# Keys and queries loaded in runs of four rows, heads split over even and odd partitions

## The chip, the core and the metric

The kernel runs on one core of one Trainium2 chip. The metric is the device time of one execution in microseconds; the median of the runs shown is what counts. TensorE is PE in the profile, its weight loads are PEld, VectorE is DVE, ScalarE is ACT, GpSimd is POOL and SyncE is SP, which here does nothing but issue DMAs.

## What is computed

Attention with a narrow window and block summaries, then a mixture of experts with one expert for each token. Cut to what matters here:

```python
B, H, S, D = 4, 8, 768, 64            # q, k, v: [B, H, S, D], float32
block, window = 32, 16
k_sum = k.reshape(B, H, nb, block, D).max(axis=3)
scores_l = scale * q @ k.T             # kept where |i - j| < window
scores_s = scale * q @ k_sum.T + log(block)
a = softmax(concat(scores_l, scores_s))
x = a @ concat(v, v_sum)               # [B*S, H*D] = [3072, 512]
e = argmax(x @ w_gate)                 # one expert of 8 for each row
out = gate * sigmoid(x @ w_og)[e] * relu(x @ w1[e]) @ w2[e]
```

## The kernel before

**Tiling.** Attention runs over 24 tiles of 128 tokens, six for each of the four batch entries. Keys and queries are loaded 256 tokens at a time: twelve loads of keys and twelve of queries, 512 KB each, called `lk.n` and `lq.n` in the order table (n = 3b + u). A load (`load`, L343) puts tokens 2p and 2p+1 of all eight heads on partition p, so that one contiguous run in DRAM is two rows of 64 float32, 512 bytes. A copy on POOL, DVE or ACT (`reorder`, L352, `rk` and `rq`) brings the row index ahead of the head index.

**Turning.** Scores need keys and queries with the head dimension on partitions. `transposed` (L407, `pk` and `pq`) makes four PE transposes into one PSUM bank `pt` of shape 128 x 2 x 256: two head pairs, 256 tokens each. Bank g holds head pairs 2g and 2g+1. ACT or DVE then copy the bank into `KT` or `QT` (`keep_k` L416, `keep_q` L436, `kk` and `kq`), and DVE takes the maximum over each 32 keys (`max_k` L424, `mk`). Every load is turned in two banks, g = 0 and g = 1.

**Scores.** `scores` (L447, `sc`) walks over head pairs 0, 1, 2, 3; each takes four products of 64 queries with 120 columns of keys, which reach 32 columns into the next 64-token block.

**What sets the order.** The order of all attention work is written out by hand in the table `ORDER`: words are executed in turn, and each engine gets its instructions in that order. All loads of k, q and v, the stores of x to DRAM (`st`, L518) and later the weight loads stand in one queue, SP's. A DMA signals its landing on one of eight semaphores, dealt out in turn, and the ninth DMA after another on the same semaphore waits for that one to have landed. Raw keys have three buffers (`rawk`), raw queries two (`rawq`).

**Afterwards.** Expert work starts when the first lists of rows are made, at about 164 us in the profile, and takes the rest of the time. Weights come as 256 KB loads with runs of 2 KB (`raw`, 128 x 512).

Of the kernel before, what the change touches and what calls it, by code (L numbers as in the profile page):

```python
# [21 lines left out]
B, H, S, D = 4, 8, 768, 64  # L22
P = 128
HP = H // 2
# [3 lines left out]
KW = 88  # L28
PAD = 16
LW = 64  # L30
KTW = NB * KW + 2 * PAD
BANKS = "SsPpVvTM"
BUFS = {"mn": 4, "pr": 3, "pTe": 2, "pTl": 3, "xs": 4, "den": 3, "xT": 2, "ls": 2, "rawk": 3, "rawq": 2, "natk": 2, "natq": 1, "mst": 2, "km": 2, "lg": 2, "posi": 2, "y": 4}
RAWS = 5
# [12 lines left out]
SCALE = 1.0 / math.sqrt(D)  # L47
# [219 lines left out]
def in_bank(ps, bank, shape, name):  # L267
    return ps.tile(shape, F32, name=name, tag=f"bank{BANKS.index(bank)}", bufs=1)


def in_ring(pool, shape, name, tag, at, dt=F32):
    return pool.tile(shape, dt, name=name, tag=f"{tag}{at % BUFS[tag]}", bufs=1)
# [43 lines left out]
def attention(tc, const, sa, sb, st, ps, dr, q, k, v, id_sb, c_sb, wg_sb, x_dr, l_dr, rt, moe, table, begin, swap, presets):  # L316
    nc = tc.nc
    QT = [sb.tile([P, HP, 256], F32, name=f"qt{i}", tag=f"qt{i}", bufs=1) for i in range(2)]
    KT = [pool.tile([P, HP, KTW], F32, name=f"kt{i}", tag=f"kt{i}", bufs=1) for i, pool in enumerate((sa, sb))]
    VW = [pool.tile([W, NB, H, VP], F32, name=f"vw{i}", tag=f"vw{i}", bufs=1) for i, pool in enumerate((sa, sb))]  # L320
    MT = sa.tile([P, H, D], F32, name="mt", tag="mt", bufs=1)

    def clear(i, k, e):
        t, x = ((KT[i][:, :, 0:PAD], 0.0), (KT[i][:, :, KTW - PAD:KTW], 0.0), (VW[i][0:PAD, 0, :, 0:D], 0.0),
                (VW[i][96:W, NB - 1, :, 0:D], 0.0), (VW[i][:, :, :, D:D + 1], 1.0),
                (VW[i][LW:LW + NS, NB - 1, :, 0:D], 0.0), (VW[i][LW:W, NB - 4:NB - 1, :, 0:D], 0.0))[k]
        (nc.vector if e == "v" else nc.gpsimd).memset(t, x)

    def evac(dst, src, scale=None, engine="a"):
        if engine == "v" and scale is None:  # L330
            nc.vector.tensor_copy(dst, src)
        elif engine == "v":
            nc.vector.tensor_scalar(dst, src, scale, None, ALU.mult)
        else:
            nc.scalar.activation(dst, src, AF.Copy, scale=1.0 if scale is None else scale)
# [3 lines left out]
    def bank(shape, name):  # L339
        return in_bank(ps, banks_of.pop(0), shape, name)  # L340

    raws, nat = {}, {}

    def load(kind, b, u):
        src = {"k": k, "q": q}[kind]
        raw = in_ring(sa if kind == "k" else sb, [P, H, 2, D], f"raw_{kind}{b}{u}", "raw" + kind, 3 * b + u)
        nc.sync.dma_start(
            raw.rearrange("p h j d -> p h (j d)"),
            src[b, :, 256 * u:256 * (u + 1), :].rearrange("h (p j) d -> p h (j d)", j=2))
        raws[kind, b, u] = raw  # L350

    def reorder(kind, b, u, engine="p"):  # L352
        t = in_ring(sa if kind == "k" else sb, [P, 2, H, D], f"nat_{kind}{b}{u}", "nat" + kind, 3 * b + u)
        r = raws.pop((kind, b, u)).rearrange("p h j d -> p j h d")
        if engine == "a":
            nc.scalar.activation(t, r, AF.Copy)
        else:
            {"v": nc.vector, "p": nc.gpsimd}[engine].tensor_copy(t, r)
        nat[kind, b, u] = t
# [45 lines left out]
    ms, km, mps, banks = {}, {}, {}, {}  # L405

    def transposed(kind, b, u, g):  # L407
        n = nat[kind, b, u]
        pt = banks[kind, b, u, g] = bank([P, 2, 256], f"{kind}tr{b}{u}{g}")
        for x in range(2):  # L410
            hp = 2 * g + x
            for j in range(2):
                nc.tensor.transpose(pt[:, x, ds(j, P, 2)],
                                    n[:, j, 2 * hp:2 * hp + 2, :].rearrange("p h d -> p (h d)"), id_sb)

    def keep_k(b, u, g, e):  # L416
        pt = banks["k", b, u, g]
        at = PAD + 4 * u * KW
        src = pt.rearrange("p x (i s) -> p x i s", s=64)
        dst = KT[b % 2][:, 2 * g:2 * g + 2, at:at + 4 * KW].rearrange("p x (i w) -> p x i w", w=KW)  # L420
        evac(dst[:, :, :, 0:48], src[:, :, :, 0:48], engine=e)
        evac(dst[:, :, :, 48 + NS:KW], src[:, :, :, 48:64], engine=e)

    def max_k(b, u, g):  # L424
        if b not in km:
            km[b] = in_ring(sb, [P, HP, NS], f"km{b}", "km", b)
        nc.vector.tensor_reduce(out=km[b][:, 2 * g:2 * g + 2, 8 * u:8 * u + 8],
                                in_=banks["k", b, u, g].rearrange("p x (n s) -> p x n s", s=32), axis=AX.X, op=ALU.max)

    def k_sum(b, engine="p"):  # L430
# [3 lines left out]
            {"v": nc.vector, "p": nc.gpsimd}[engine].tensor_copy(own, km[b][:, hp, :].unsqueeze(1).to_broadcast([P, NB, NS]))  # L434

    def keep_q(b, u, g, e):  # L436
        evac(QT[(3 * b + u) % 2][:, 2 * g:2 * g + 2, :], banks["q", b, u, g], -SCALE, e)

    lg_sb = {}

# [204 lines left out]
    def key(f, kind=None):  # L645
        return (lambda s, *x: f(kind, s // 3, s % 3, *x)) if kind else (lambda s, *x: f(s // 3, s % 3, *x))

    work = {
        "cl": clear, "lk": key(load, "k"), "lq": key(load, "q"), "rk": key(reorder, "k"), "rq": key(reorder, "q"),
        "lv": lambda t, x, q: load_vw(*tiles[t], (x,), nc.gpsimd if q == "p" else nc.sync),  # L650
        "pk": key(transposed, "k"), "kk": key(keep_k), "mk": key(max_k), "pq": key(transposed, "q"), "kq": key(keep_q), "ks": k_sum,
        "me": means, "ke": keep_means, "mg": gather_means, "kg": keep_gathered, "pu": put_means,
        "sc": scores, "ma": mask, "mi": smallest, "su": subtract, "ex": exps, "tp": turn_p, "kp": keep_p, "va": values, "no": norm,
# [7 lines left out]
    for w in order:  # L661
        w, _, at = w.partition(":")
# [687 lines left out]
```

## Time and profile before

| | us |
|---|---|
| median of 3 runs | 498.84 |
| lowest and highest | 498.22 and 499.87 |
| profiled execution, its own time | 501.86 |
| its span, first to last instruction | 500.1 |
| PE busy in the span | 474.1 |
| DVE, ACT, POOL busy | 363.7, 313.7, 178.9 |

The profiled execution took 3.0 us longer than the median. A page of the profile gives the busy time of each engine, the busy share in 40 slices with the granted TensorE clock, the DMA engines' share and rate, the chain of work that ended last, and the costliest groups of instructions. The trace behind it can be asked for single waits, for the DMA traffic of a stretch, and for the queue of SP. A busy PE is not a PE at its peak, since ends of matmuls are modelled; what counts is where it waits and for whom.

### The profile page before, as it was taken

The page shows a single profiled execution, that of the slowest core. Times are in us where ns is not written, and L with a number is a line of the kernel's source. Part 1 is how long each engine was busy: PE and PEld are TensorE (multiplying, and loading weights), DVE is VectorE, ACT ScalarE, POOL GpSimd, SP SyncE. Part 2 cuts the span into 40 slices and gives each one's busy share as a digit, 9 for nine tenths or more (in the row PEclk, how much of TensorE's full clock was granted, in tenths as well). Part 3 has the DMA queues.
Part 4 walks back from the last instruction along what each step waited for, and adds up shares of the span by engine and source line. Part 5 has one row for each costly group of instructions (what it writes and reads, how often), then busy time and mean ns, then how long its engine had stood idle before and what let it go on. Part 6 is the DMA issues. An engine that isn't in the chain of part 4 may idle for free.

```text
span 500.1 us, 12189 instructions
## 1 busy us (share of the span) xinstructions
PE 474.1 (95%) x4146; PEld 388.2 (78%) x4146; DVE 363.7 (73%) x819; ACT 313.7 (63%) x635; POOL 178.9 (36%) x194
## 2 busy tenths in 40 slices
PE   9889999987699999889999999999999999999994
PEld 8757787863588875879888888888888888888872
DVE  5979799785488546785778777887878599889510
ACT  3386687874396536164667677786867579769410
POOL 2575775445637258803040111112131312303110
PEclk9999999997799999979999999999999999999999
DMA  9996997978067538908878666858676679968601
GB/s 237 200 193 139 287 223 177 261 150 229 27 204 264 154 98 282 382 14 299 295 225 272 205 195 229 272 164 280 179 266 206 212 216 304 318 213 272 229 3 51
DMA packets 109962, 105.33 MB, mean 211 GB/s; under 512 B 47929, under 2 KB 72891, under 8 KB 109884
## 3 DMA queue, kind: packets, MB, share of 16 engines
q1 hardware_dynamic: 104588, 91.78, 63.8%
q0 software_dynamic: 5296, 12.62, 7.0%
q8 instruction: 36, 0.59, 0.5%
q14 instruction: 42, 0.34, 0.2%
HBM read 93.08 MB, written 13.46 MB: 213 GB/s over the span
## 4 chain that ended last, share of the span: by engine, by line
PE 66%; DMA 15%; issue 7%; DVE 5%; SPq 3%; ACT 1%; POOL 1%; POOLq 0%; ACTq 0%; DVEq 0%
DMA out_dram<-y,lst 9%; PE hp L971 8%; PE yp L1219 7%; PE yp L1217 7%; PE yp L1218 7%; PE hp L969 5%; PE pv L500 3%; PE hp L1046 3%; SPq L369 3%; PE yp L1060 3%; PE hp L967 3%; PE sp L454 3%; PE pt L486 2%; DMA raw_k<-in_k_dram 2%; DMA raw_q<-in_q_dram 2%
## 5 line engine op out<-in xcount | busy, mean ns | idle before, releaser
L930 DVE TENSOR_TENSOR w2l<-raw,w2h 128x512 fp32r<-128x512 f32 x101 | 70.6, 717 | 21.8 <-ACT w2h L929 19.4
L929 ACT ACTIVATE w2h<-raw 128x512 fp32r<-128x512 f32 x104 | 64.6, 631 | 26.2 <-PE yp L1219 18.3
L891 POOL DMA_INDIRECT xg<-x_dr,lst x30 | 35.5, 1184 | 122.3 <-PE xp L941 104.0
L1217 PE MATMUL yp<-w2h,hh 128*128 128x512 f32 x192 | 76.8, 400 | 0.0
L1218 PE MATMUL yp<-w2l,hh 128*128 128x512 f32 x192 | 75.8, 395 | 0.0
L1219 PE MATMUL yp<-w2h,hl 128*128 128x512 f32 x192 | 74.9, 395 | 0.2
L930 DVE TENSOR_TENSOR w1l<-raw,w1h 128x512 fp32r<-128x512 f32 x99 | 66.1, 695 | 6.9 <-ACT w1h L929 3.6
L1245 POOL DMA_INDIRECT out_dram<-y,lst x26 | 27.5, 1059 | 106.5 <-DVE y L1242 32.1
L929 ACT ACTIVATE w1h<-raw 128x512 fp32r<-128x512 f32 x104 | 62.0, 625 | 3.2 <-PE hp L967 1.5
L971 PE MATMUL hp<-xhl,w1h 128*128 128x512 f32 x216 | 62.1, 395 | 0.0
L476 POOL TENSOR_TENSOR pr<-pr,mn 128x960 f32<-128x960 f32 x24 | 43.3, 1810 | 28.9 <-DVE mn L471 14.3
L969 PEld LDWEIGHTS hp<-xhl,w1l 128*128 128x128 f32 x288 | 44.3, 189 | 5.9
L969 PE MATMUL hp<-xhl,w1l 128*128 128x256 f32 x288 | 46.1, 281 | 0.0
L1219 PEld LDWEIGHTS yp<-w2h,hl 128*128 128x128 f32 x192 | 36.3, 190 | 8.7 <-DVE hl L1133 1.0
L981 ACT ACTIVATE hh<-hs 128x256 fp32r<-128x256 f32 x72 | 29.8, 414 | 21.1 <-DVE hs L974 17.8
L1217 PEld LDWEIGHTS yp<-w2h,hh 128*128 128x128 f32 x192 | 36.6, 191 | 7.3
L1218 PEld LDWEIGHTS yp<-w2l,hh 128*128 128x128 f32 x192 | 36.5, 190 | 7.3
L464 DVE TENSOR_TENSOR pr<-sp,c_sb 128x480 f32<-128x480 f32 x48 | 29.0, 651 | 14.0 <-PE sp L454 5.1
L982 DVE SCALAR_TENSOR_TENSOR hl<-hs,hh 128x256 fp32r<-128x256 f32 x72 | 30.3, 422 | 11.9 <-ACT hh L981 11.4
L971 PEld LDWEIGHTS hp<-xhl,w1h 128*128 128x128 f32 x216 | 35.8, 189 | 3.2
L974 DVE TENSOR_TENSOR hs<-hp,hs 128x256 f32<-128x256 f32 x72 | 30.3, 421 | 9.9 <-ACT hs L973 6.4
L500 PEld LDWEIGHTS pv<-vw,pT 120*64 120x64 f32 x768 | 26.5, 142 | 12.2 <-issue 10.1
(215 smaller groups left out, 945.9 us busy)
## 6 DMA issues: line engine op xcount, KB each, us to landing
raw<-in_moe_w_dram SPq DMA_DIRECT2D x224, 256.0 KB
raw_k<-in_k_dram SPq DMA_DIRECT2D x12, 512.0 KB
raw_q<-in_q_dram SPq DMA_DIRECT2D x12, 512.0 KB
x_dr<-xs SPq DMA_DIRECT2D x24, 256.0 KB
vw<-in_v_dram SPq DMA_DIRECT2D x44, 128.0 KB
vw<-in_v_dram SPq DMA_DIRECT2D x44, 64.0 KB
w1l<-in_moe_w_dram SPq DMA_DIRECT2D x8, 256.0 KB
w2l<-in_moe_w_dram SPq DMA_DIRECT2D x8, 256.0 KB
```

What stands on the lines that cost most here:

```text
L476: nc.gpsimd.tensor_tensor(pr, pr, mns.pop(i).unsqueeze(2).to_broadcast([P, H, W]), ALU.subtract)
L500: nc.tensor.matmul(po[64 * y:64 * y + 64, h % 4, :], lhsT=pTs[i][:, h % 2, h // 2, 64 * y:64 * y + 64], rhs=VW[b % 2][:, 2 * tok + y, h, 0 ...
L891: nc.gpsimd.indirect_dma_start(out=self.xg[t], out_offset=None, in_=self.x_dr[0:rows, :], in_offset=bass.IndirectOffsetOnAxis(ap=self.list ...
L929: nc.scalar.activation(hi, raw, AF.Copy)
L930: (lo_by or nc.vector).tensor_tensor(lo, raw, hi.bitcast(F32), ALU.subtract)
L969: nc.tensor.matmul(hp[:, 0, :], lhsT=w_l[c], rhs=self.xh[:, c, :], start=False, stop=False)
L971: nc.tensor.matmul(hp, lhsT=w_h[c], rhs=self.xhl[:, c], start=False, stop=c == NC - 1)
L974: nc.vector.tensor_tensor(hs, hp[:, 0, :], hs, ALU.add)
L982: nc.vector.scalar_tensor_tensor(hl[:, j, :], hs, 0.0, hh[:, j, :].bitcast(F32), ALU.max, ALU.subtract)
L1217: nc.tensor.matmul(y, lhsT=hh[:, j, tk], rhs=w_h, start=j == 0, stop=False)
L1218: nc.tensor.matmul(y, lhsT=hh[:, j, tk], rhs=w_l, start=False, stop=False)
L1219: nc.tensor.matmul(y, lhsT=hl[:, j, tk], rhs=w_h, start=False, stop=j == NF - 1)
```

## The change

One load becomes two DMAs. Partition 2n+g now takes tokens 4n to 4n+3 of heads 4g to 4g+3: g = 0 fills the even partitions with heads 0 to 3, g = 1 the odd ones with heads 4 to 7. A contiguous run in DRAM is four rows, 1 KB, and there are 512 runs in a load instead of 1024. A transpose takes row j and two neighbouring heads of each partition; its 128 output columns alternate between head pair g (from the even partitions) and head pair g+2 (from the odd ones). Bank g so holds head pairs g and g+2, and the copies out of it write every second head pair. Counts of transposes, copies and maxima are the same; the order table is the same.

```diff
-        raw = in_ring(sa if kind == "k" else sb, [P, H, 2, D], f"raw_{kind}{b}{u}", "raw" + kind, 3 * b + u)
-        nc.sync.dma_start(
-            raw.rearrange("p h j d -> p h (j d)"),
-            src[b, :, 256 * u:256 * (u + 1), :].rearrange("h (p j) d -> p h (j d)", j=2))
+        raw = in_ring(sa if kind == "k" else sb, [P, HP, ROWS, D], f"raw_{kind}{b}{u}", "raw" + kind, 3 * b + u)
+        part = src[b, :, 256 * u:256 * (u + 1), :].rearrange("(g h) (p j) d -> g p h (j d)", g=2, j=ROWS)
+        for g in range(2):
+            nc.sync.dma_start(raw[ds(g, 64, 2)].rearrange("p h j d -> p h (j d)"), part[g])
...
-        for x in range(2):
-            hp = 2 * g + x
-            for j in range(2):
-                nc.tensor.transpose(pt[:, x, ds(j, P, 2)],
-                                    n[:, j, 2 * hp:2 * hp + 2, :].rearrange("p h d -> p (h d)"), id_sb)
+        for j in range(ROWS):
+            nc.tensor.transpose(pt[:, :, ds(j, P // 2, ROWS)].rearrange("p g n -> p n g"),
+                                n[:, j, 2 * g:2 * g + 2, :].rearrange("p h d -> p (h d)"), id_sb)
...
-        dst = KT[b % 2][:, 2 * g:2 * g + 2, at:at + 4 * KW].rearrange("p x (i w) -> p x i w", w=KW)
+        dst = KT[b % 2][:, ds(g, 2, 2), at:at + 4 * KW].rearrange("p x (i w) -> p x i w", w=KW)
...
-        evac(QT[(3 * b + u) % 2][:, 2 * g:2 * g + 2, :], banks["q", b, u, g], -SCALE, e)
+        evac(QT[(3 * b + u) % 2][:, ds(g, 2, 2), :], banks["q", b, u, g], -SCALE, e)
```

The same step of two stands in the output of `max_k` and, as `[P, ROWS, HP, D]` for `[P, 2, H, D]`, in the copy of `reorder`.

SP's queue near its start, before the change (raw_k00 is the first load of keys, raw_q00 the first of queries, vw0 a tile of values, DMAHW0 to 7 the eight landing semaphores):

```order
L347 DMA raw_q00_282<-in_q_dram 128x8x128
L347 DMA raw_q01_353<-in_q_dram 128x8x128
L219 DMA c_sb_67<-in_cst_dram 128x679
L347 DMA raw_k10_376<-in_k_dram 128x8x128 [waits DMAHW0_49,Pool_49]
L369 DMA vw0_92<-in_v_dram 64x8x64
L369 DMA vw0_92<-in_v_dram 64x8x64 [waits DMAHW1_49]
L347 DMA raw_k11_394<-in_k_dram 128x8x128 [waits DMAHW2_49,Pool_49]
L347 DMA raw_q02_415<-in_q_dram 128x8x128 [waits DMAHW4_49,DMAHW3_49,Activation_49]
```

And with the change, the same place:

```order
L350 DMA raw_q00_285<-in_q_dram 64x4x256
L350 DMA raw_q00_285<-in_q_dram 64x4x256 [waits DMAHW0_49]
L350 DMA raw_q01_357<-in_q_dram 64x4x256 [waits DMAHW1_49]
L350 DMA raw_q01_357<-in_q_dram 64x4x256 [waits DMAHW2_49]
L220 DMA c_sb_67<-in_cst_dram 128x679 [waits DMAHW3_49]
L350 DMA raw_k10_381<-in_k_dram 64x4x256 [waits DMAHW4_49,Pool_49]
L350 DMA raw_k10_381<-in_k_dram 64x4x256 [waits DMAHW5_49]
L370 DMA vw0_92<-in_v_dram 64x8x64 [waits DMAHW6_49]
L370 DMA vw0_92<-in_v_dram 64x8x64 [waits DMAHW7_49]
L350 DMA raw_k11_400<-in_k_dram 64x4x256 [waits DMAHW0_49,Pool_49]
```

Each load takes two places and two semaphores, so a wait for an earlier landing comes after four loads instead of eight.

On PE the rows keep their places. What moves is where a wait stands in a tile of scores, here the fourth tile (`sc.3`), whose second key block reaches into keys that ACT copies late (`kk.2.1.a`). Before, the last eight of its 16 products (kt0 and qt1 are the turned keys and queries, sp030 and sp031 the two banks of scores):

```order
L454 MATMUL sp031_487<-kt0_90,qt1_89 64x120
L454 MATMUL sp030_486<-kt0_90,qt1_89 64x120
L454 MATMUL sp031_487<-kt0_90,qt1_89 64x120
L454 MATMUL sp030_486<-kt0_90,qt1_89 64x120 [waits Activation_49]
L454 MATMUL sp031_487<-kt0_90,qt1_89 64x120
L454 MATMUL sp030_486<-kt0_90,qt1_89 64x120
```

With the change, the products around the wait, which now is the seventh of the tile instead of the eleventh:

```order
L453 MATMUL sp030_495<-kt0_90,qt1_89 64x120
L453 MATMUL sp031_496<-kt0_90,qt1_89 64x120
L453 MATMUL sp030_495<-kt0_90,qt1_89 64x120 [waits Activation_49]
L453 MATMUL sp031_496<-kt0_90,qt1_89 64x120
L453 MATMUL sp030_495<-kt0_90,qt1_89 64x120
```

Four products (eight passes in the trace, which shows each as two) have moved behind that wait.

## Rows read from the trace of the kernel before

**Rows 1.** The page: span, PE's busy time, busy tenths of the DMA engines in 40 slices.

```profile
span 500.1 us, 12189 instructions
PE 474.1 (95%) x4146; PEld 388.2 (78%) x4146; DVE 363.7 (73%) x819; ACT 313.7 (63%) x635; POOL 178.9 (36%) x194
DMA  9996997978067538908878666858676679968601
```

**Rows 2.** Chain that ended last, to 200 us: start, duration (us), what.

```profile
14.89 10.22 DMA raw_q<-in_q_dram
...
48.46 5.70 DMA raw_k<-in_k_dram
54.18 1.12 DVE nat_k L358
...
94.22 6.75 DMA raw_k<-in_k_dram
101.03 1.05 POOL nat_k L358
```

**Rows 3.** Timelines of ACT, DVE and PE: start, duration, instruction [idle before <- ended by].

```profile
25.19 1.06 ACT L356 ACTIVATE nat_q<-raw_q 128x1024 f32<-128x1024 f32 x1 [1.83 <-DMA raw_q<-in_q_dram]
...
27.43 0.69 DVE L331 COPY pT<-pt 120x512 f32<-120x512 f32 x1 [1.59 <-PE pt L486]
...
54.18 1.11 DVE L358 COPY nat_k<-raw_k 128x1024 f32<-128x1024 f32 x1 [1.09 <-DMA raw_k<-in_k_dram]
...
23.25 0.63 PE L454 MATMUL sp<-kt,qt 64*64 64x120 f32 x12 [0.86 <-ACT kt L335]
...
26.30 0.66 PE L413 MATMUL qtr<-id_sb,nat_q 128*128 128x128 f32 x4 [1.85 <-ACT nat_q L356]
...
55.44 1.06 PE L413 MATMUL ktr<-id_sb,nat_k 128*128 128x128 f32 x8 [0.35 <-DVE nat_k L358]
...
102.12 0.66 PE L413 MATMUL ktr<-id_sb,nat_k 128*128 128x128 f32 x4 [1.43 <-POOL nat_k L358]
```

**Rows 4.** SP's queue, timeline: start, time of the issue, DMA.

```profile
8.85 0.37 SPq L347 DMA_DIRECT2D raw_k<-in_k_dram  x1
...
11.98 2.80 SPq L347 DMA_DIRECT2D raw_k<-in_k_dram  x1
14.89 2.71 SPq L347 DMA_DIRECT2D raw_q<-in_q_dram  x1
...
40.57 4.48 SPq L369 DMA_DIRECT2D vw<-in_v_dram  x7
```

**Rows 5.** DMA traffic of 6.33 to 9.93 us, all but 31 packets 512 B.

```profile
DMA  9999999999999999999999999999999999999999
DMA packets 2072, 1.05 MB, mean 290 GB/s; under 512 B 31, under 2 KB 2072, under 8 KB 2072
```

**Rows 6.** DMA traffic of 150.2 to 155 us, nearly all packets 2 KB.

```profile
DMA packets 1053, 1.90 MB, mean 396 GB/s; under 512 B 133, under 2 KB 133, under 8 KB 1052
```

**Rows 7.** DMA traffic of 21 to 23.5 us: values, 64 partitions, 256-B packets.

```profile
DMA  8999999999999999999999999999999997999999
GB/s 197 209 250 229 242 209 238 254 246 221 221 172 180 184 176 135 123 111 131 115 111 131 111 90 107 127 94 107 131 127 152 119 111 66 123 115 90 74 82 53
DMA packets 1448, 0.37 MB, mean 149 GB/s; under 512 B 1396, under 2 KB 1448, under 8 KB 1448
```

**Rows 8.** Groups by shape, PE to 150 us, ACT to 165 us: count, busy us, mean ns.

```profile
L486 PE MATMUL pt<-id_sb,pr 128*120 128x128 f32 x160 | 22.1, 280 | 0.0
L413 PE MATMUL ktr<-id_sb,nat_k 128*128 128x128 f32 x96 | 13.5, 276 | 2.4 <-POOL nat_k L358 2.1 <-DVE nat_k L358 0.3
L335 ACT ACTIVATE qt<-qtr 128x512 f32<-128x512 f32 x23 | 13.2, 596 | 15.3 <-PE qtr L413 15.2
L335 ACT ACTIVATE xT<-xtr 128x512 f32<-128x512 f32 x16 | 9.2, 598 | 3.4 <-PE xtr L524 3.2
```

**Rows 9.** Busy time in stretches: PE, PEld, DVE, ACT, POOL, clock, DMA share, GB/s.

```profile
20.00:25.00 5.00, 3.60 (x79) 2.80 (x76) 4.48 (x7) 2.21 (x5) 4.80 (x4) 1.00 1.06 160
```

More of the change, by code (lines that the diff above doesn't have):

```diff
@@ L31 @@
 KTW = NB * KW + 2 * PAD
+ROWS = 4
 BANKS = "SsPpVvTM"
@@ L345, in load @@
         src = {"k": k, "q": q}[kind]
-        raw = in_ring(sa if kind == "k" else sb, [P, H, 2, D], f"raw_{kind}{b}{u}", "raw" + kind, 3 * b + u)
-        nc.sync.dma_start(
-            raw.rearrange("p h j d -> p h (j d)"),
-            src[b, :, 256 * u:256 * (u + 1), :].rearrange("h (p j) d -> p h (j d)", j=2))
+        raw = in_ring(sa if kind == "k" else sb, [P, HP, ROWS, D], f"raw_{kind}{b}{u}", "raw" + kind, 3 * b + u)
+        part = src[b, :, 256 * u:256 * (u + 1), :].rearrange("(g h) (p j) d -> g p h (j d)", g=2, j=ROWS)
+        for g in range(2):
+            nc.sync.dma_start(raw[ds(g, 64, 2)].rearrange("p h j d -> p h (j d)"), part[g])
         raws[kind, b, u] = raw
     def reorder(kind, b, u, engine="p"):
-        t = in_ring(sa if kind == "k" else sb, [P, 2, H, D], f"nat_{kind}{b}{u}", "nat" + kind, 3 * b + u)
+        t = in_ring(sa if kind == "k" else sb, [P, ROWS, HP, D], f"nat_{kind}{b}{u}", "nat" + kind, 3 * b + u)
         r = raws.pop((kind, b, u)).rearrange("p h j d -> p j h d")
@@ L426, in max_k @@
             km[b] = in_ring(sb, [P, HP, NS], f"km{b}", "km", b)
-        nc.vector.tensor_reduce(out=km[b][:, 2 * g:2 * g + 2, 8 * u:8 * u + 8],
+        nc.vector.tensor_reduce(out=km[b][:, ds(g, 2, 2), 8 * u:8 * u + 8],
                                 in_=banks["k", b, u, g].rearrange("p x (n s) -> p x n s", s=32), axis=AX.X, op=ALU.max)
```

## The prediction

> **What bounds the kernel now.** I read the page first, then the chain of waits, then the timelines around each transfer in it, then the DMA traffic of single stretches. The page says that PE is busy for 95% of the span and that the DMA engines are nearly full in the first slices and loosely filled later [rows 1]. A busy share does not say what a load of keys or queries is worth; the chain does. It goes through such a load at three places: one issued at 14.89 us that is used at 25.19, one issued at 48.46 and used at 54.18, one issued at 94.22 and used at 101.03 [rows 2]. Behind each stands a wait of a compute engine. At 25.19 ACT had been idle for 1.83 us for the third load of queries, PE then had waited 1.85 us for ACT, and DVE 1.59 us for PE. At 54.18 DVE had waited 1.09 us, but PE only 0.35. At 102.12 PE had waited 1.43 us for a copy of keys [rows 3]. Together PE lost 1.85 + 0.35 + 1.43 = 3.63 us to keys and queries at those places. That is about all the change can win on the path, since between them PE and DVE have work without such gaps, and after about 164 us, in the expert work, no key or query is loaded.
>
> What paces these loads? Between 6.33 and 9.93 us the DMA engines were full with 512-B packets and moved 290 GB/s [rows 5]. SP is held back by them: an issue takes 0.37 us when there is room, but 2.71 and 2.80 us in the stretch before the first wait [rows 4]. So the first eight loads stand in a queue that the transfer rate empties.
>
> **Part 1: the packets (gain).** A load is 524 KB. At 290 GB/s it takes 1.81 us. Rows with 1 KB don't exist in this trace, so I bound them: no better than the 2-KB packets at 396 GB/s [rows 6], 1.32 us; no better than now would be 1.81. Between the two I assume a fixed cost for a packet and one for a byte. On 16 engines a 512-B packet takes 512 x 16 / 290 = 28.2 ns, a 2-KB packet 2048 x 16 / 396 = 82.7 ns; 1 KB lies a third of the way, 46.4 ns, 353 GB/s, and the load takes 1.49 us. That is 0.32 us less for each, if a transfer to 64 partitions in steps of two runs as one to 128 does. Worse is possible too, and that is the bound on the other side: from 21 to 23.5 us the engines were as full with 64-partition loads of values and moved 149 GB/s [rows 7], by which a load would take 3.52 us. I take 1.49 us: the row with 149 GB/s has 256-B packets, mostly for partitions 0 to 63, where the new halves have 1 KB and reach across all 128.
>
> **Part 2: a second issue (cost).** 24 more DMAs stand in SP's queue. An issue with room costs 0.37 us [rows 4], say 0.4 with what lies between two. Two issues take 0.8 us, less than the 1.49 us that the data takes, so wherever loads stand one behind another the second issue is covered. Where values follow, seven loads of values pass in 4.48 us, 0.64 us each [rows 4], and there one more issue is 0.4 us for whatever is queued behind it: values, stores of x and the next keys. Against that a load has half as many packets to be made, so that the issue behind it should be held back for a shorter time. Bounds: 0 and 0.4 us for each load outside the first stretch; I take 0, as the 2.71 and 2.80 us are the transfer's and not the issue's. The waits for semaphores come after eight half loads instead of eight loads. Eight halves are four loads, 4 x 1.49 = 6.0 us of transfers still queued, so the engines don't run dry while SP waits for a landing.
>
> **Part 3: columns that alternate (unknown, taken as nothing).** 24 loads x 8 transposes = 192 transposes write their columns in turn to the left and the right half of a bank. The trace has transposes of keys with step 2 in the output (mean 276 ns) and of probabilities with step 1 (280 ns) [rows 8]: a step costs nothing there. No row alternates over 1 KB. A gain is excluded, since count and columns are the same. As the upper bound a transpose takes twice its pace: eight took 1.06 us at 55.44 [rows 3], so 0.13 us more for each. I take 0, the value of the nearest rows, which are the same instruction into the same memory.
>
> **Part 4: copies to every second head pair.** ACT writes a query bank in one piece in 596 ns and the turned x, in four pieces, in 598 ns [rows 8]. So 0. The copies of raw data read 16 runs of 64 numbers before and after: 0.
>
> **Part 5: scores meet their late keys earlier.** Bank 1 held head pairs 2 and 3; now it holds 1 and 3. In the fourth tile 12 passes stood behind the wait for ACT's copy and took 0.63 us [rows 3]; now 20 do. Eight passes more, at 0.63 / 12 each, are 0.4 us. Behind them on PE stand the turns of probabilities and then of the queries just named. Cost 0.4 us, once.
>
> **The sum.** At 25 us, eight loads have passed: 8 x 0.32 = 2.6 us earlier, of which ACT and PE can use 1.8 before their own work is late; less the 0.4 of part 5 is 1.4. At 54 us the loads are another four by 0.32 ahead, but PE waits only 0.35: 0.35. At 102 us, the load is issued behind a store that waits for DVE, so it can't be issued earlier than that; its own transfer and one ahead of it in the queue are 0.32 shorter each; with landing delays I take 0.3. Sum 1.4 + 0.35 + 0.3 = 2.05 us. All of it lies before the expert work, which is a stream of PE work that starts when the last scores are done, so I carry it to the end. The profiled execution took 501.86 us; by this sum it becomes 499.8. It stands 3.0 us above the median, with no wait that explains it, so the sum is taken off the median: 498.84 - 2.05 = 496.8.
>
> **Rivals.**
> *Half loads get in each other's way.* Mechanism: transfers whose rows go to 64 partitions make DMA engines share ways into the memory, so all engines are busy and less arrives. Speaking for it: in one stretch the rate falls from about 230 to about 100 GB/s with the engines still full, with nothing but 64-partition loads in it [rows 7]. Against it: small packets, one half of the partitions, and the loads here reach across all 128. Price: halfway between 1.49 and 3.52 is 2.5 us, 0.7 more than now; eight loads give 5.5 us at the first wait, where nothing covers it, and later ones some 1 us. With half of that, 0.35 a load, about 3.5 us: 502.3. The point from which it decides is a load of 1.81 us. The Trainium skill has a rule against this change: in "DMA: Bandwidth & Descriptors", section "Rules for kernel authors", it advises against two transfers to disjoint partition halves, which run one after the other on the same 16 engines, and for one of 128 partitions; "SBUF — State Buffer", section "Door 1: The DMA port swizzle", says that partitions 0 to 63 reach only half of the ports. By the first the time would be that of the next rival; no run here shows it for alternate partitions. With the second the trace agrees for the lower half of the partitions, at 149 GB/s [rows 7].
> *The gain is hidden.* The load arrives earlier, but ACT or DVE are late next, or a lagging engine holds the landing. For it: DVE was busy for 4.48 of the 5 us from 20 to 25 [rows 9], and the load of 14.89 us takes 10.22 us to its use though its own data takes 1.8 [rows 2, 5]. The time is that of before less 0.65 us, the two smaller terms of the sum, or plus 0.4 us, part 5 alone: 498.2 to 499.2.
> *Alternate columns cost.* 192 x 0.13 = 25 us of PE time; if half of it lies where others wait for PE, 12 us: 511. The trace has nothing for it.
> *It does not do what it says:* runs stay 512 B inside the queue. Then two issues and no gain, within the second rival's figures.
>
> **How the numbers follow.** Forecast as summed: 0.42. Hidden, or nothing changed inside the queue: 0.31. Half loads slower: 0.22. Columns: 0.05. The likeliest is the forecast, 496.8. The low end has the three PE waits gone entirely, and 0.4 us, one issue, for values that wait behind fewer packets: 498.84 - 3.63 - 0.4 = 494.8. The high end takes in the halves at 0.35 us more, 502.3; above it lie the upper part of that rival and the columns, some 0.13, and below the low end 0.05. A measurement of this kernel can tell about 0.3%, 1.5 us, from no change. Faster by more than that: most of the forecast's case, 0.39. Within: the rest of it and the hidden case, 0.34. Slower: 0.27.
>
> **What would show it.** Right: between 6 and 10 us packets of 1 KB at about 350 GB/s; SP's issue of the third load of queries some 2 us earlier; ACT's wait of 1.83 us before its copy gone, PE's wait of 1.85 us below 0.5, eight transposes still in 1.06 us. Wrong: the DMA engines full at 290 GB/s or less in that stretch; the wait at 25 us as long or longer; transposes longer; or everything earlier at 60 us and the end where it was.

## The result and the profile after

The changed kernel took 502.13 us (median of 14 runs, 499.04 to 504.77) against 498.82 us for the kernel before on the same chip (14 runs, 496.05 to 503.64): a ratio of 1.0055, interval 1.0029 to 1.0080. By this comparison it is slower by about 2.7 us, where 2 us less were forecast. Four more comparisons, below, gave ratios of 0.9977 to 1.0007, so the loss of 0.55% stands alone; in none of the five did the forecast gain of 0.4% show clear of the noise. (Medians here are over all runs; the ratios leave disturbed ones out, so that the two can differ by some tenths of a per cent.)

The page of the changed kernel: span, PE's busy time, busy tenths of the DMA engines. The profiled execution took 502.75 us.

```profile
span 500.7 us, 12228 instructions
PE 473.7 (95%) x4146; PEld 388.1 (77%) x4146; DVE 362.6 (72%) x819; ACT 313.8 (63%) x635; POOL 178.9 (36%) x194
DMA  7997799977167438907878666858685678879401
```

Against [rows 1] the first slice (12.5 us) has 7 where 9 stood: the engines are no longer full there. The DMA traffic of 6.33 to 9.93 us, the stretch of [rows 5]; the last row is packets, MB and the time of the packets as a share of 16 engines' time:

```profile
DMA  9989997778989798955655799788999999999999
DMA packets 1103, 1.07 MB, mean 296 GB/s; under 512 B 63, under 2 KB 1103, under 8 KB 1103
q1 hardware_dynamic: 1103, 1.07, 91.3%
```

A packet now has 1 KB and takes 0.913 x 16 x 3.6 us / 1103 = 47.7 ns. (This counts the time of the packets; the 46.4 ns of the prediction are bytes over rate, a measure that comes out somewhat lower: on [rows 5] it gives 28.2 ns, and the packets' share of 116.4% in the same window of before gives 1.164 x 57.6 us / 2072 = 32.4 ns.) And yet only 296 GB/s arrive, six more than before, because the engines have gaps. SP's queue shows whose gaps they are (start, time of the issues, DMA, count):

```profile
0.75 1.41 SPq L350 DMA_DIRECT2D raw_k<-in_k_dram  x2
...
2.85 2.58 SPq L350 DMA_DIRECT2D raw_k<-in_k_dram  x4
5.47 2.59 SPq L350 DMA_DIRECT2D raw_q<-in_q_dram  x4
8.11 0.62 SPq L220 DMA_DIRECT2D c_sb<-in_cst_dram  x1
...
13.95 1.93 SPq L350 DMA_DIRECT2D raw_q<-in_q_dram  x2
...
46.67 1.28 SPq L350 DMA_DIRECT2D raw_q<-in_q_dram  x2
47.99 1.27 SPq L350 DMA_DIRECT2D raw_k<-in_k_dram  x2
```

Four halves take 2.58 us: 0.65 us each, and no less at 46.67, where there is room (1.28 for two); a whole load took 0.37 us [rows 4]. From 0.75 us to the third load of queries SP issues almost without a break, and that load goes out at 13.95, only 0.94 us ahead of the 14.89 of [rows 4].

Timelines of ACT and PE (idle time before, and what ended it, in brackets), in the places of [rows 3], the last at a new one. The third PE line, at 56.42, is the turn of the keys that stood at 55.44 before:

```profile
23.36 1.06 ACT L357 ACTIVATE nat_q<-raw_q 128x1024 f32<-128x1024 f32 x1 [1.12 <-DMA raw_q<-in_q_dram]
...
22.12 0.83 PE L453 MATMUL sp<-kt,qt 64*64 64x120 f32 x20 [0.55 <-ACT kt L336]
...
24.47 0.65 PE L412 MATMUL qtr<-id_sb,nat_q 128*128 128x128 f32 x4 [0.93 <-ACT nat_q L357]
...
56.42 1.06 PE L412 MATMUL ktr<-id_sb,nat_k 128*128 128x128 f32 x8 [3.01 <-DVE nat_k L359]
...
151.41 1.61 PE L499 MATMUL pv<-vw,pT 120*64 120x65 f32 x46 [1.57 <-POOL vw L402]
```

The first wait shrinks: PE turns the queries at 24.47 instead of 26.30. At 56.42 the lead is gone and more: PE waits 3.01 us for keys, where it waited 0.35 before. The wait of 1.43 us at 102 [rows 3] is absent, and at 151 there is one of 1.57 us for values, which the trace of before does not have. By 166 us it cancels: the same products of the experts (L1046 before, L1045 now) start at 166.13 before and at 166.12 now. The chain shows the late keys:

```profile
14.79 8.47 DMA raw_q<-in_q_dram
...
48.65 6.83 DMA raw_k<-in_k_dram
55.58 0.70 DVE nat_k L359
```

The second half of these keys was issued at 48.65, later than the whole load before (48.46, [rows 2]), though the queries in front of it went out 1.35 us earlier (46.67 against 48.02). Two loads now cost four issues. And from there it took 6.83 us until it was used, instead of 5.70.

So the two profiled executions, 502.75 and 501.86 us, hardly differ, and neither shows the 2.7 us. They show a gain and a loss of the same size. How large either is differs from execution to execution: in the four other profiles of the changed kernel (a1 to a4 below) PE waits 1.9, 1.8, 1.1 and 1.2 us for the third queries and turns them at 25.4 to 26.0 us, so the 24.47 of this one is the earliest of five.

### The profile page after: what moved, and what is told of

It reads as the page before. It is cut to its first block, busy times and chain, and to the rows that moved or that the text cites. A ratio compares the mean times of both kernels' runs of the same rounds, so it can differ in the third digit from the quotient of the medians.

```text
span 500.7 us, 12228 instructions
## 1 busy us (share of the span) xinstructions
PE 473.7 (95%) x4146; PEld 388.1 (77%) x4146; DVE 362.6 (72%) x819; ACT 313.8 (63%) x635; POOL 178.9 (36%) x194
## 4 chain that ended last, share of the span: by engine, by line
PE 56%; DMA 16%; issue 15%; DVE 5%; POOL 3%; SPq 3%; ACT 1%; POOLq 1%; ACTq 0%; DVEq 0%
DMA out_dram<-y,lst 9%; PE hp L970 6%; PE yp L1216 5%; PE yp L1218 5%; PE yp L1217 5%; PE hp L968 4%; PE pv L499 3%; PE hp L1045 3%; PE pt L485 3%; PE yp L1059 3%; PE sp L453 2%; SPq L370 2%; PE hp L966 2%; PE hp L978 2%; DMA raw_q<-in_q_dram 2%
## 5 line engine op out<-in xcount | busy, mean ns | idle before, releaser
L499 PE MATMUL pv<-vw,pT 120*64 120x65 f32 x768 | 30.2, 230 | 6.4 <-issue 4.4
```

What stands on the lines that cost most here:

```text
L499: nc.tensor.matmul(po[64 * y:64 * y + 64, h % 4, :], lhsT=pTs[i][:, h % 2, h // 2, 64 * y:64 * y + 64], rhs=VW[b % 2][:, 2 * tok + y, h, 0 ...
```

## The experiments

The theories on what takes the gain back: **A**, SP's time for the second issue; **B**, that halves to 64 partitions end late or slow; **C**, the alternating columns; **D**, the rows of 1 KB themselves. Beside them, for the first ratio alone: low-clock stretches of TensorE that fell unevenly. Ratios are against the kernel before, run on the same chip beside each.

| kernel | median us | before | ratio (interval) |
|---|---|---|---|
| b1, before again | 483.5 | 485.61 | 0.9976 (0.9937 to 1.0015) |
| a1, changed again | 481.83 | 485.61 | 0.9991 (0.9950 to 1.0032) |
| a2, changed again | 482.67 | 483.55 | 0.9977 (0.9947 to 1.0008) |
| a3, changed again | 483.29 | 483.38 | 0.9997 (0.9968 to 1.0026) |
| a4, changed again | 499.01 | 499.29 | 1.0007 (0.9971 to 1.0042) |
| c_two, before with two issues | 485.34 | 485.61 | 1.0014 (0.9983 to 1.0046) |
| e_one, changed with one issue | 481.17 | 485.61 | 0.9922 (0.9890 to 0.9954) |
| e2, the same | 479.1 | 483.55 | 0.9884 (0.9829 to 0.9940) |
| e3, the same | 498.63 | 499.29 | 0.9979 (0.9945 to 1.0013) |
| i_dummy, e_one and an idle issue | 484.46 | 483.38 | 1.0017 (0.9979 to 1.0055) |
| h_four, changed with four issues | 507.62 | 483.55 | 1.0487 (1.0429 to 1.0545) |
| d_halves, neighbouring partitions | 492.97 | 483.55 | 1.0155 (1.0083 to 1.0227) |
| f_cols, before with the columns | 483.69 | 483.38 | 0.9985 (0.9948 to 1.0022) |

**One issue for each load (e_one, e2).** Even and odd partitions can be filled by one transfer: ahead of the token the head counts through all eight, and head 4 begins where the next partition does.

```diff
-        part = src[b, :, 256 * u:256 * (u + 1), :].rearrange("(g h) (p j) d -> g p h (j d)", g=2, j=ROWS)
-        for g in range(2):
-            nc.sync.dma_start(raw[ds(g, 64, 2)].rearrange("p h j d -> p h (j d)"), part[g])
+        part = src[b, :, 256 * u:256 * (u + 1), :].rearrange("(g h) (p j) d -> p g h (j d)", g=2, j=ROWS)
+        nc.sync.dma_start(raw.rearrange("p h j d -> p h (j d)"), part)
```

> The changed kernel with one transfer for each load instead of two, same 1-KB runs and the same places. Theory A (second issue): the loss is gone, SP issues a load in 0.37 to 0.46 us and the wait at 25 us is gone too: 0.993 to 0.999 of before. Theory B (half loads): also better than the changed kernel, since no transfer goes to 64 partitions. Theory C (columns) or D (1-KB rows): as slow as the changed kernel, 1.0055.

> The changed kernel with one transfer for each load, again (0.9922 in its first comparison). Theory A (the second issue takes back what the packets give): 0.990 to 0.996 of before again, and better than a2 by 0.3 to 0.7%. If the first ratio was luck: within 0.3% of a2.

0.9922 and 0.9884: faster than before by 3.8 and 5.6 us, in the sense of theory A and by more than the ranges expected, and theory D falls. (Against b1's runs of the kernel before, on the first of the two chips, the medians differ by 0.5%.) Against the changed kernel on the same chips the ratios lie 0.7 and 0.9% lower, the medians 0.1 and 0.7%. The profiled executions set them further apart: the first products of the experts (`hp`) start at 149.52 and 149.20 us in e_one and e2, at 152.61 and 154.84 in a1 and a2. DMA traffic of e_one from 6.33 to 9.93 us:

```profile
DMA packets 1296, 1.29 MB, mean 359 GB/s; under 512 B 34, under 2 KB 1296, under 8 KB 1296
q1 hardware_dynamic: 1296, 1.29, 109.2%
```

SP's queue:

```profile
12.22 1.65 SPq L349 DMA_DIRECT2D raw_q<-in_q_dram  x1
...
28.19 0.62 SPq L349 DMA_DIRECT2D raw_k<-in_k_dram  x1
```

And ACT's copy of the third queries:

```profile
22.65 1.06 ACT L356 ACTIVATE nat_q<-raw_q 128x1024 f32<-128x1024 f32 x1 [0.69 <-DMA raw_q<-in_q_dram]
```

With one issue the engines are full again and move 359 GB/s; a packet takes 1.092 x 57.6 us / 1296 = 48.5 ns, no other than in halves. The third queries go out at 12.22 instead of 14.89, ACT's wait for them falls from 1.83 to 0.69 us, and PE has none. In the same 14 us from the start the engines have moved 3.67 MB, against 3.47 in the changed kernel and 3.44 before. That an issue of this form also takes 0.62 us, where 0.37 to 0.46 were expected, shows that the halving does not make an issue cheaper: the time goes with the issue, not with its bytes.

**The second issue alone (i_dummy).** e_one, and behind each load a transfer of 1 KB that nothing uses.

```diff
+        extra = const.tile([P, 4], F32, ...)
+        nc.sync.dma_start(extra[ds(0, 64, 2)], src[b, 0, 0:64, 0:4])
```

> The kernel with one transfer for each load (0.9922, 0.9884), and behind each load a second transfer of 1 KB to 64 partitions that nobody uses: the second issue alone, without halving the load. Theory A (SP's time for the second issue is what the changed kernel loses): as a1 and a2, 0.995 to 1.001 of before, PE waits some 1.8 us for queries at 25 us again. Theory B (half loads end later on single DMA engines): as the kernel with one transfer, 0.988 to 0.993.

1.0017 (0.9979 to 1.0055), at the upper end of what theory A expects: with hardly a byte more the whole gain is gone. SP's queue:

```profile
12.54 0.97 SPq L349 DMA_DIRECT2D raw_k<-in_k_dram  x1
13.55 3.03 SPq L351 DMA_DIRECT2D xk<-in_k_dram  x1
16.68 0.60 SPq L349 DMA_DIRECT2D raw_q<-in_q_dram  x1
```

PE:

```profile
25.86 0.66 PE L413 MATMUL qtr<-id_sb,nat_q 128*128 128x128 f32 x4 [1.20 <-ACT nat_q L358]
```

The third queries go out at 16.68, 4.5 us later than in e_one. Part of that is an issue held for 3.03 us: an extra issue costs its 0.62 us and can also be the one that is held back by the data in front. PE's wait was 1.2 us and not the 1.8 expected; that miss is of size only. One thing this run does not separate: the idle transfer also takes one of the eight landing semaphores, and to 16 us SP waits three times for an earlier landing, 1.3 us together. In the five profiles of the changed kernel no such wait stands in that stretch, nor in that of h_four below, so there it is the issues themselves.

**Four issues (h_four).** Each half split again by head pairs, packets and places unchanged.

```diff
-            nc.sync.dma_start(raw[ds(g, 64, 2)]..., part[g])
+            for i in range(2):
+                nc.sync.dma_start(raw[ds(g, 64, 2)][:, 2 * i:2 * i + 2]..., part[g][:, 2 * i:2 * i + 2])
```

> The changed kernel with each half load split again, by head pairs: four transfers of 128 KB for each load, the same 1-KB packets to the same places. Theory A (each issue takes 0.62 us of SP): 48 more issues, 16 of them ahead of the load used at 25 us, so up to 16 x 0.66 = 10 us later there less what the data takes anyway: 1.005 to 1.02 of a2, PE's wait for those queries 3 us or more. Theory B (what matters is which partitions a transfer reaches): the same as a2 within 0.3%.

1.0487 (1.05 of a2), more than theory A's upper figure of 1.02. SP's queue:

```profile
4.14 5.16 SPq L351 DMA_DIRECT2D raw_k<-in_k_dram  x8
```

DMA traffic of 6.33 to 9.93 us:

```profile
DMA packets 779, 0.73 MB, mean 203 GB/s; under 512 B 80, under 2 KB 778, under 8 KB 778
```

PE's waits to 160 us (total, times, longest):

```profile
PE ktr L414 <- POOL nat_k L361: 7.4, 5, 2.8
PE qtr L414 <- POOL nat_q L361: 4.3, 3, 2.4
```

5.16 us for eight issues of 131 KB are 0.645 us each and 203 GB/s, and 203 GB/s is what the engines moved. SP's pace is the rate. In the changed kernel the same pace allows 262 KB / 0.645 us = 406 GB/s, just over what the packets can use, and any small transfer in the queue pushes it below. PE waits at eight places for keys and queries; the estimate had counted the one at 25 us alone, and that one did not come: ACT copies the third queries at 27.53 us without a wait. The eight waits are 11.7 of the 24 us. The granted clock was lower too (0.91 in four of the seven stretches of 20 us between 20 and 160 us); how much of the rest that makes was not worked out.

**Two issues with the old packets (c_two).** The kernel before, each load as two transfers to even and odd partitions.

```diff
-        nc.sync.dma_start(
-            raw.rearrange("p h j d -> p h (j d)"),
-            src[b, :, 256 * u:256 * (u + 1), :].rearrange("h (p j) d -> p h (j d)", j=2))
+        part = src[b, :, 256 * u:256 * (u + 1), :].rearrange("h (n g j) d -> g n h (j d)", g=2, j=2)
+        for g in range(2):
+            nc.sync.dma_start(raw[ds(g, 64, 2)].rearrange("p h j d -> p h (j d)"), part[g])
```

> The kernel before with its 512-B runs and its columns, only each load of keys and queries issued as two transfers, to the even and to the odd partitions. Theory A (second issue) and theory B (half loads) both: slower than before, ratio 1.005 or more, since nothing is gained from the packets (the wait at 25 us stays at 1.8 us or grows). Theory C (alternating columns): 1.000. Theory D (1-KB rows themselves): 1.000. Between A and B: by A the two issues take 1.3 us on SP together and the packets land as before behind that; by B the load's last packets come 1 us or more behind the rest on single DMA engines.

1.0014, where 1.005 or more was expected; against b1 on the same chip the medians differ by 485.34 / 483.5 = 0.4%. With 512-B packets the data takes longer than two issues, so most of the second is hidden. The comparison alone would not separate the theories; it agrees with A and excludes a large B.

**Neighbouring partitions (d_halves).** Heads 0 to 3 to partitions 0 to 63, 4 to 7 to 64 to 127.

```diff
-            nc.sync.dma_start(raw[ds(g, 64, 2)]...
+            nc.sync.dma_start(raw[64 * g:64 * g + 64]...
-            nc.tensor.transpose(pt[:, :, ds(j, P // 2, ROWS)].rearrange("p g n -> p n g"),
+            nc.tensor.transpose(pt[:, :, ds(j, P // 2, ROWS)],
```

> The changed kernel with heads 0 to 3 on partitions 0 to 63 and 4 to 7 on 64 to 127 instead of even and odd ones; a turn's columns then don't alternate. Theory A (issue count): the same as a2 within 0.3%, SP issues of 0.62 us. Theory C (columns): faster than a2. Theory B (64 neighbouring partitions take turns at the memory): slower than a2 by 0.5% or more, packets far over 46 ns.

1.0155: here theory B holds. DMA traffic of 6.33 to 9.93 us:

```profile
DMA packets 812, 0.78 MB, mean 217 GB/s; under 512 B 48, under 2 KB 812, under 8 KB 812
q1 hardware_dynamic: 812, 0.78, 113.6%
```

The engines are full and move 217 GB/s; a packet of the same 1 KB takes 1.136 x 57.6 us / 812 = 80.6 ns instead of 47.7. So the split over even and odd partitions is what keeps the halves from getting in each other's way. The trace agrees with the Trainium skill ("SBUF — State Buffer", section "Door 1: The DMA port swizzle"), by which 64 neighbouring partitions reach half of the ports; by its formula for the port, even ones over all 128 reach all.

**Columns alone (f_cols).** The kernel before with `ds(2 * x + j, P // 2, 4)` over both head pairs instead of `ds(j, P, 2)` in one.

> The kernel before, with the columns of its transposes alternating between two head pairs as in the changed kernel and nothing else changed, so that heads are mixed in the scores: the values computed are others, the instructions and their sizes the same. Theory C (columns cost): slower by up to 25 us, a transpose over 276 ns. Otherwise 1.000 within 0.4%, 276 ns.

0.9985, and the groups of key transposes (count, busy us, mean ns), of f_cols to 110 us:

```profile
L413 PE MATMUL ktr<-id_sb,nat_k 128*128 128x128 f32 x96 | 13.9, 281 | 0.2 <-POOL nat_k L358 0.2
```

Of the changed kernel to 165 us:

```profile
L412 PE MATMUL ktr<-id_sb,nat_k 128*128 128x128 f32 x96 | 13.5, 275 | 3.2 <-DVE nat_k L359 3.0
```

And of b1 to 150 us:

```profile
L413 PE MATMUL ktr<-id_sb,nat_k 128*128 128x128 f32 x96 | 13.9, 281 | 0.9 <-POOL nat_k L358 0.7 <-PE warmer L643 0.2
```

281 in both kernels of the faster chips, 275 against 276 [rows 8] on the first: columns cost nothing. Theory C falls.

**The same kernels again (b1, a1 to a4, e3).** These were for the first ratio itself.

> The kernel before, unchanged, as a control. Every theory: ratio 1.000 within 0.003. Its granted clocks tell whether the changed kernel's 0.975 to 0.988 in its runs is lower than before's: if the 2.7 us come from more stretches at the lower clock level, before's mean clock should lie some 0.005 to 0.01 higher (one such stretch of 6.8 us at half pace is 0.0068 of the mean clock and up to 3.4 us); if not, the clocks should be alike.

> The changed kernel, unchanged, as a control: ratio 1.003 to 1.008 again, and a second profile. Theory A (two issues of 0.62 us for each load instead of one of 0.37 to 0.46 us make loads late that stand behind values) and theory B (half loads end late on single DMA engines): the load of keys issued at 48.65 us is used at 55 us again, PE waits some 3 us for it. If that wait is below 1 us in this profile, the late landing was an accident of one execution.

> The changed kernel again, unchanged. It was 1.0055 in its first comparison (clock 0.975 to 0.988, three stretches of 6.8 us at the lower level in the profiled execution) and 0.9991 in the second (clock 0.993 to 0.999, at most one such stretch ahead of the end). If the first loss belongs to the kernel, 1.003 to 1.008 again wherever the clock is low; if it came from where such stretches fell, 0.995 to 1.002 with before's and this kernel's clocks alike.

> The changed kernel again, for the clocks beside it. If the first ratio of 1.0055 belongs to executions with three long stretches at the lower clock, it comes back only where the mean clocks are near 0.98; at 0.99 and above 0.995 to 1.002.

> The changed kernel again, with the clocks of the kernel before beside it. If its first ratio, 1.0055, comes from the kernel at a low clock, it is 1.003 or more where the mean clock of both is near 0.98. If it comes from one stretch at the lower clock more in the changed kernel's executions, the ratio over 1.003 stands only where its clock lies some 0.007 under that of the kernel before, at about 3 us for each 0.007. At a clock over 0.99 in both: 0.997 to 1.001, as in the three comparisons so far.

> The kernel with one transfer for each load, beside a4 on the same chip. Theory A (the second issue takes back the gain): 0.4 to 1.2% faster than a4, whatever the clock. If low-clock stretches decide, its distance to a4 changes sign or size with the difference of their clocks, by 3 us for each 0.007.

a1 missed what was expected of it in both parts: its ratio came out at 0.9991 instead of 1.003 to 1.008, and its wait for the keys at 55 us was 0.3 us instead of some 3. By its own test a wait as long as 3.01 us was an accident of one execution; a3 and a4, with 1.5 and 1.3 us, have it smaller.

The chips fall into two kinds. On three of them the kernel before takes 483 to 486 us at mean clocks of 0.987 to 0.999, on the chips of the first comparison and of a4 some 499 us; a4's chip had 0.971 to 0.989 for both kernels. PE and its granted clock from 110 to 140 us, of a1 (PE busy and instructions, clock, DMA share, GB/s):

```profile
110.00:140.00 30.00, 26.88 (x508) 1.00 0.78 246
```

And of a4:

```profile
110.00:140.00 30.00, 24.36 (x298) 0.77 0.44 132
```

A clock of 0.77 over this stretch is a mean of the 2.4 and 1.2 GHz levels. On the slower chips PE pauses there with nothing that it waits for in the trace, and does 298 instructions where a1 does 508. Both kernels have it in the same way (before's trace: 281 instructions, 0.77), so it belongs to the distance between the chips and not to the one between the kernels: of the 17 us between a4 and a1, 11 stand at the first products of the experts (163.77 and 152.61 us).

a4 was the test for low clocks, as its chip is of the slower kind: 1.0007, with mean clocks of 0.983 and 0.981 (before) over the runs. So a low clock as such does not bring the first ratio back. That one more low-clock stretch fell into the first 14 runs was expected to be worth 3 us, which would be the size; but of the clocks of before's runs there only the profiled one is on record (0.979, the changed kernel's 0.978), so this was not tested. **What made the first comparison differ by 0.55% stays open.**

e3 went against what theory A expects in size: 0.9979 and only 0.1% under a4, not 0.4 to 1.2%. In its profile PE has no wait for keys or queries over 0.3 us to 160 us, and it turns the keys at 53.41 us where a4 does at 55.07, much as e_one (53.33). At the first products of the experts it is 1.3 us ahead (162.51 and 163.77), less than the 3.1 and 5.6 us of the faster chips; why the medians of the 12 runs hardly show it was not settled.

## Why the prediction was wrong

**The packets were right.** 46.4 ns and 353 GB/s were worked out; e_one has 359 GB/s, which by the same measure is 1024 x 16 / 359 = 45.6 ns. By eight loads of 0.32 us the third queries would be there 2.6 us earlier, and in e_one ACT copies them 2.5 us earlier (22.65 for 25.19). That the two are so close is partly luck: e2 and e3 copy them at 23.08 and 23.84, where they are no longer what ACT waits for. The gain is there for a kernel that can feed the engines.

**The second issue is the step that failed.** It was put at 0.37 to 0.4 us with two issues hidden under 1.49 us of data, and taken as nothing. The price came from a row of another form of transfer, though [rows 4] also has 0.64 us for each load of values, which goes to 64 partitions or fewer: the halves take 0.65 us, two of them 1.3. And cover was counted load by load, while SP's queue also holds other loads (`id_sb` and two of values with 0.26 MB together, `c_sb` with 0.35 MB), each 0.6 us. Summed over the queue the 18 issues ahead of the third queries take the 13.2 us from 0.75 to 13.95 almost without a gap, against 7 x 1.49 = 10.4 us for the data of the keys and queries; with the other 0.61 MB at e_one's 359 GB/s it is an estimated 12.1. e_one has 11 issues there and is through at 12.22. The Trainium skill has both sides: "DMA: Bandwidth & Descriptors", section "Rules for kernel authors", advises one 128-partition transfer instead of two disjoint halves, and the runs agree (0.9922 against 0.9991 on one chip), though by SP's issues and not by the reason given there, that the halves run one after the other: their packets were no slower. The same page's section "Issuing engines are not separate DMA queues" calls the time to start a transfer usually small beside the transfer; here 0.65 us stand beside 0.74, half of the 1.49 above.

**Columns and copies were right** at nothing (275 against 276 ns; ACT's copies of a query bank 596 ns in both).

**The earlier wait of the scores was right in kind, too large in size.** 20 passes now stand behind ACT's copy and take 0.83 instead of 0.63 us, 0.2 and not 0.4; and the wait itself shrank from 0.86 to 0.55.

**The sum.** At 25 us PE gained 1.83 us in the profiled execution where 1.4 were forecast. At 54 us 0.35 were to be won and 2.66 were lost (a wait of 3.01 for 0.35). At 102 us 1.43 came instead of 0.3: the load that the prediction held fixed at 94.22 went out at 91.85. At 151 us a wait of 1.57 us for values appeared that no step had; with before's loads it stands there too in other executions (0.76 us in b1, 0.47 in f_cols). "Carried to the end" thus held for none of the terms alone; the working stopped at the loads that waited before, and did not ask which load would be late next. For the keys used at 56 us that answer depends on the execution: in the five profiles of the changed kernel PE waits 3.0, 0.3, 0, 1.5 and 1.3 us for them, in the three with one transfer not at all.

**The rivals.** "Half loads get in each other's way" named the time that was measured, 502.3, but not by a mechanism of this kernel, so that the time lies inside the stated range is luck: its packets are as fast in halves as in whole loads. Where that mechanism exists, in d_halves, its price was close: 524 KB at 217 GB/s are 2.4 us, and 2.5 were priced. "The gain is hidden" had PE, ACT or a lagging engine as the cover; of the four later comparisons (0.9977 to 1.0007 of 498.8 are 497.7 to 499.1) three fall within its 498.2 to 499.2 and a2 lies just below, with SP in the place of those engines. Neither had SP as the bound.

## What to carry to other kernels

Larger packets pay only as far as the issuing queue keeps up: count all issues of the queue in a stretch, small ones too, by the row of the same form, and compare their sum with that of the data. If a layout seems to need two transfers, look for an order of the dimensions that makes it one: here that turned a change that gave nothing into one that is 0.8 and 1.2% faster than the kernel before on two chips and 0.2%, which its interval does not tell from nothing, on a third; its median is below the changed kernel's on all three. When a load gets earlier, work out which load is late next before the gain is carried to the end.

## What the runs showed of the hardware

An issue on SP took 0.60 to 0.65 us for halves of 64 partitions whether they moved 1, 131 or 262 KB, and for e_one's whole load of 524 KB (0.75 for the first of a run), but mostly 0.37 to 0.46 us, where there was room, for the whole load in the form of before. What in the form sets this was not tried.

A wait of PE can cost twice. PE, its clock and traffic from 26 to 30 us, of b1:

```profile
26.00:30.00 4.00, 3.62 (x18) 0.57 0.76 164
```

And of e_one:

```profile
26.00:30.00 4.00, 4.00 (x62) 1.00 0.75 124
```

In b1 PE had waited 2.1 us for the queries, and then most of the next 4 us ran at 1.2 GHz; e_one had no such wait and kept 2.4 GHz. The same stretch had a clock of 0.66, 0.50, 0.50 and 0.61 in a1, a2, c_two and f_cols, behind waits of 1.9, 1.8, 2.2 and 1.8 us for these queries. The wait does not always bring this: the profiled execution of before had waited 1.85 us and ran on at 1.00.
